# A fused convolution and two-token expert kernel: constants stored by piece, the router's two largest found together, longer weighting and transform sums, and a new order

## The chip, the cores and the metric

The kernel runs on one core of a Trainium2 chip. A core has five engines that run their own instruction streams: TensorE (PE, matmuls into PSUM), VectorE (DVE), ScalarE (ACT), GpSimd (POOL) and SyncE (SP, which here only issues DMAs). Engines meet through semaphores. The metric is device time in microseconds (us) of one execution, lower is better.

## The reference

`L` is 2048 tokens, `D` 512 channels, `NS` 128 states per channel. A gate `g` mixes two branches of the same input `u`: a long convolution (an S4 layer) and an expert layer that touches two tokens alone.

```python
dt = exp(log_dt)[:, None];  A = A_re + 1j * A_im
P  = exp((dt * A)[:, :, None] * l)                      # l = 0 .. L-1, per channel and state
K  = einsum("dn,dnl,dn->dl", C, P, dt * B).real         # kernel of the convolution, [D, L]
a  = irfft(rfft(pad(u)) * rfft(pad(K)))[:L] + u * Dskip # causal convolution over tokens

r   = x @ w_r;  idx = argsort(-r)[:2]                   # the two tokens with the largest logits
y   = (silu(x[idx] @ w_gate) * (x[idx] @ w_up)) @ w_down * sigmoid(r[idx])
b   = x.at[idx].add(y)

g   = sigmoid((u * gate_w).sum(-1))
out = g * a + (1 - g) * b                               # [1, 2048, 512] bf16
```

## The kernel before, in words

The kernel is a list of operations made by `P.add` (through the helpers `TT`, `TS`, `STT`, `CP`, `EV`, `AF`, `MM`, `DMA`), each with the buffers that it reads and writes. `PLAN` gives the order in which they are emitted, each with the alternative (mostly: which engine) that is used, and `BANKS` gives each PSUM tile its banks. `replay` and `emit_plan` turn that into one stream per engine, with a semaphore wait for every dependence that crosses engines. So every engine runs in the fixed order of `PLAN`, and one late operand holds up all that stands behind it on its engine. The costs in the helpers (`c_dve`, `issue`, `rate` and so on) describe operations to the planner that made `PLAN`; they emit nothing.

The channels go in two halves of 256 (`hf` or `c`, 0 and 1). The stages, with the names used below:

- **Parameters** (`nat0` to `nat5`, `ldt`, `al`, `bs`, `bn`, `bc`, `kw`, `k0`, and "polar"): the parameters are loaded, transposed on PE (`nt`, `nw`) and brought to modulus and phase. `hm` are 22 warm-up matmuls on a constant written by `one`.
- **Exponentials** (`ep`, `eq`, `ek` on ACT) give the moduli; `moduli` (`cm`) and `weigh` (`mw`, `mf`) multiply them up on DVE.
- **Coarse and fine waves** (`coarse`, `fine`): PE adds up a phase in PSUM (`pa`, L683 and L688), ACT takes its sine (`sin`, L437), and DVE multiplies by the moduli: `ns`, `pi`, `pr` for each of 4 coarse groups, `qm` (L729) for each of 5 fine groups G_. Each `qm` covers 2048 columns: real and imaginary plane of 1024.
- **Lags** (`lags`): PE multiplies coarse by fine waves (`kmm`, L925), which are evicted (`kae`), selected (`sel`, L939) and evicted again (`kce`, `kcx`, `k0c`). `kt` and `ku` make the tail terms.
- **Spectrum** (`spectrum`): PE multiplies the lags by the constant `c_near`, four pieces of 512 KB (`kn`, L1145; `ks`, L964), and `c_far` (`kf`, L969); the results are evicted (`khe`, `khf`).
- **Transform** of the input (`transform(m)`, m the block of 1024 tokens): PE multiplies tokens by the constant `c_fwd`, two pieces of 512 KB for odd and even tokens (`fl`, `fm`, L553; `fw`, L872). Evictions are `fwo` (scaled by -2, L861) and `fwe`. Two accumulating DMAs on POOL's queue (`vb`) and then DVE's `v1`, `v0`, `w1`, `w0` (L886 to L890) form the planes. `w1` and `w0` are four operations of 1024 columns per block, one for each plane.
- **Products and inverse** (`products(c, j)`, `inverse(c, j)`): DVE multiplies input and kernel spectra (`prod`) and sums them (`acc`, `yr`, `yi`, `pq`, `b0`, `b2`, `b13`), in places with the sums on PE (`ac`, L1032 to L1036, evicted by `ace`). PE does the inverse (`iv`, L1111 to L1116), with the second branch added through `rd` (the residual), and `ive` (L1127, L1131) evicts and weighs by the gate; `out` stores.
- **Rows** (L732 to L844): logits of the gate and the router come from a transposed load of the input (`xt`) by `wl` and `log`. The router follows, then the gather of its two tokens (`gu`), the expert (`wg`, `wu`, `wd`, `ff`, `dn`), `z1`, `bu`, and the scatter (`sc`) into `u_routed`, a copy of the input in device memory made by `uc`. From it `ue` and `u2` are loaded for `rd`'s matmuls.

The router before finds its two maxima one after the other (L776 to L783). `gmax` reduces 16 columns to one per partition (L769), spreads that over all partitions by a matmul (`gt`, L771) and reduces 128 columns (L772). For each of the two tokens it runs twice: for the logit, then for the index among the places where the logit is found (`cand`). Between the two tokens the first one's place is masked (`sel`, `mask`). Then `rs0`, `msb`, `ix0` (POOL) and `idx` (DVE) bring the logits to the sigmoid and the indices to an integer.

Half 0 of each stage runs ahead of half 1, with the transform and the rows between. On SP the input, `c_fwd`, the transposing load, the expert's weights, the constants of the spectrum and the stores follow each other in `PLAN`'s order.

## Time and profile before

| | |
|---|---|
| three runs | 148.18, 149.94 and 154.42 us; median 149.94 |
| profiled execution | 148.89 us, span of its instructions 146.8 us, mean granted TensorE clock 0.977 |
| bytes moved | 26.40 MB, mean 180 GB/s |
| engine instructions, busy | in the prediction below |

The page's strip of the span in 40 slices shows how full each engine is (a digit is the busy share in tenths, 9 is 90% or more):

```profile
PE   7964669999999959998999976599999998999992
PEld 3751363445446626665558664587788666877881
DVE  0789999889999989999999998999999979999943
ACT  4699999899999859888978777999968943358461
POOL 4000000604944583631500000000000000000000
PEclk9999985699999999999999999999999999999999
DMA  4799999995089992189970559248751000002155
```

PE is TensorE's matmuls and PEld its weight loads, which run beside them. Each digit stands for 3.67 us. A row such as `L408 DVE TENSOR_TENSOR RB<-RB 128x2048 bf16<-128x2048 bf16 x60 | 71.0, 1218 | ...` gives line, engine and operation, destination and source with partitions x elements, the count, the time in all (us), the mean of one (ns), and behind the second bar the idle time of the engine just before with what ended it. Nearly all buffers lie in one allocation, `RB`, so shapes and lines tell operations apart. L408, L414, L425, L428, L434 and L437 are lines of helpers that record many operations.

### The profile page before, as it was taken

Reading aid. Unit: us, or ns where it says so; the run is one execution under the profiler, and the core shown is the slowest. Engines: PE = TensorE matmul, PEld = TensorE weight load, DVE = VectorE, ACT = ScalarE, POOL = GpSimd, SP = SyncE. Lnnn points to the kernel's source line nnn. Section 1 sums busy time; section 2 is a strip of 40 time slices with the busy share of each in tenths; the row PEclk is TensorE's granted clock in tenths of the full one; section 3 lists DMA queues with packets and bytes.
Section 4 is the critical chain, followed back from the end, with each engine's and each line's share of the span. In section 5 each row is a group of like instructions: output and inputs, shape, how many; then the busy total and the mean of one; then the engine's idle time right before and its main releaser. Section 6 shows DMA issues by size and latency. Waiting matters only on the chain.

```text
span 146.8 us, 3150 instructions
## 1 busy us (share of the span) xinstructions
PE 129.1 (88%) x1302; PEld 89.1 (61%) x1309; DVE 132.9 (91%) x172; ACT 116.4 (79%) x165; POOL 25.6 (17%) x34
## 2 busy tenths in 40 slices
PE   7964669999999959998999976599999998999992
PEld 3751363445446626665558664587788666877881
DVE  0789999889999989999999998999999979999943
ACT  4699999899999859888978777999968943358461
POOL 4000000604944583631500000000000000000000
PEclk9999985699999999999999999999999999999999
DMA  4799999995089992189970559248751000002155
GB/s 133 208 264 262 292 220 357 408 401 228 9 133 180 193 369 63 36 241 262 474 333 29 156 94 424 110 136 291 289 108 49 0 4 0 0 0 76 38 168 154
DMA packets 23501, 26.40 MB, mean 180 GB/s; under 512 B 9208, under 2 KB 19840, under 8 KB 23328
## 3 DMA queue, kind: packets, MB, share of 16 engines
q1 hardware_dynamic: 20574, 23.03, 49.5%
q0 software_dynamic: 1136, 2.26, 8.9%
q10 hardware_dynamic: 1778, 0.92, 2.1%
q8 instruction: 10, 0.16, 0.5%
q14 instruction: 3, 0.02, 0.1%
HBM read 19.78 MB, written 4.20 MB: 163 GB/s over the span
## 4 chain that ended last, share of the span: by engine, by line
PE 40%; DVE 26%; DMA 11%; ACT 11%; SPq 4%; POOL 3%; issue 2%; ACTq 0%
DVE RB L408 20%; PE psm L1116 11%; DMA RB<-in_A_u_dram 8%; ACT RB L428 7%; PE psm L964 6%; ACT RB L437 4%; PE psm L939 4%; PE psm L872 3%; DMA RB<-c_near 3%; PE psm L925 3%; PE psm L1032 3%; PE psm L1111 2%; DVE RB L434 2%; POOL RB L414 2%; PE psm L746 2%
## 5 line engine op out<-in xcount | busy, mean ns | idle before, releaser
L408 DVE TENSOR_TENSOR RB<-RB 128x2048 bf16<-128x2048 bf16 (+12 forms) x120 | 112.5, 987 | 2.7 <-PE psm L1036 1.3
L428 ACT ACTIVATE RB<-psm 128x1024 bf16<-128x1024 f32 (+7 forms) x46 | 39.4, 872 | 10.7 <-PE psm L1036 6.2
L437 ACT ACTIVATE RB<-psm 128x1024 bf16<-128x1024 int16 (+1 forms) x37 | 36.4, 1020 | 4.5 <-PE psm L541 1.4
L872 PE MATMUL psm<-RB 128*128 128x512 bf16 x61 | 17.2, 419 | 6.3 <-DVE RB L861 3.2
L1116 PE MATMUL psm<-RB 128*128 128x256 bf16 x160 | 22.1, 273 | 0.0
L683 PE MATMUL psm<-RB 128*128 128x256 f16 (+1 forms) x112 | 20.7, 326 | 0.5 <-ACT RB L437 0.4
L437 ACT ACTIVATE RB<-RB 128x512 bf16<-128x512 f32 (+5 forms) x32 | 16.5, 590 | 3.0 <-POOL RB L414 1.8
L1116 PEld LDWEIGHTS psm<-RB 128*128 128x128 bf16 x160 | 15.6, 98 | 1.9 <-ACT RB L428 0.2
L1127 ACT ACTIVATE RB<-psm,RB 128x256 bf16<-128x256 f32 x27 | 10.9, 478 | 6.9 <-PE psm L1116 6.8
L964 PE MATMUL psm<-RB 128*128 128x256 bf16 x128 | 15.0, 273 | 1.0 <-DMA RB<-c_near 0.9
L683 PEld LDWEIGHTS psm<-RB 128*128 128x128 f16 x112 | 10.3, 97 | 8.7 <-ACT RB L437 0.9
L872 PEld LDWEIGHTS psm<-RB 128*128 128x128 bf16 x64 | 6.3, 105 | 14.6 <-DVE RB L861 4.0
L964 PEld LDWEIGHTS psm<-RB 128*128 128x128 bf16 x128 | 12.4, 98 | 3.6 <-DMA RB<-c_near 1.4
L688 PE MATMUL psm<-RB 128*128 128x512 f16 x44 | 13.0, 391 | 1.3 <-ACT RB L437 1.1
L925 PE MATMUL psm<-RB 128*128 128x80 bf16 x256 | 10.2, 198 | 2.3 <-DVE RB L408 1.6
L925 PEld LDWEIGHTS psm<-RB 128*128 128x128 bf16 x256 | 9.7, 96 | 3.7 <-ACT RB L428 3.4
L428 ACT ACTIVATE RB<-psm,RB 128x1024 bf16<-128x1024 f32 (+1 forms) x9 | 9.1, 1064 | 1.2 <-PE psm L969 1.2
L1111 PE MATMUL psm<-RB 128*128 128x256 bf16 x32 | 8.7, 273 | 0.0
L1032 PE MATMUL psm<-RB 128*128 128x512 bf16 x21 | 6.5, 380 | 0.7 <-ACT RB L428 0.6
L688 PEld LDWEIGHTS psm<-RB 128*128 128x128 f16 x44 | 3.6, 98 | 5.7 <-ACT RB L437 4.5
L422 POOL CAST RB<-RB 128x16 bf16<-128x16 f32 (+3 forms) x5 | 5.6, 1123 | 8.0 <-DVE RB L761 7.9
L414 POOL TENSOR_SCALAR RB<-RB 128x1 f32<-128x1 f32 (+3 forms) x5 | 6.5, 1291 | 0.3
(75 smaller groups left out, 123.0 us busy)
## 6 DMA issues: line engine op xcount, KB each, us to landing
RB<-in_A_u_dram SPq DMA_DIRECT2D x8, 256.0 KB, 5.8
RB<-RB POOLq DMA_DIRECT2D x4, 512.0 KB, 7.2
RB<-c_near SPq DMA_DIRECT2D x4, 512.0 KB, 5.7
RB<-c_inv SPq DMA_DIRECT2D x1, 2048.0 KB, 7.9
RB<-u_routed SPq DMA_DIRECT2D x2, 1024.0 KB, 6.0
RB<-in_B_w_gate_dram SPq DMA_DIRECT2D x1, 1792.0 KB, 12.0
RB<-in_B_w_up_dram SPq DMA_DIRECT2D x1, 1792.0 KB, 15.5
RB<-in_B_w_down_dram SPq DMA_DIRECT2D x1, 1792.0 KB, 9.4
```

Source lines behind the costliest of these rows:

```text
L408: return P.add(name, [(eng, c_dve(n, mode) if eng == DVE else 1.0, lambda h: h.tensor_tensor(out=o(), in0=a_(), in1=b_(), op=op))], rd, wr ...
L428: return lambda h: h.activation(out=o(), in_=a_(), func=ACTF.Copy, scale=scale() if callable(scale) else scale)
L437: return P.add(name, [(ACT, cost or c_act(n), lambda h: h.activation(out=o(), in_=a_(), func=func, scale=scale))], rd, wr, table=table, **kw)
L683: r = h.matmul(P32(t, 0, 0, 128, 256 * l0, (1, 256 * nl)), DGM(0, 128, (DD.index(d) + 2) * 128, (1, 128)), src(0, 128, col + hf * CW, (0, ...
L688: r = h.matmul(P32(t, b, 0, 128, 0, (1, 512)), DGM(0, 128, 0, (1, 128)), DGM(0, 128, 128 + c_, (0, 512)), start=False, stop=False, skip_gr ...
L872: x = h.matmul(P32(t, b, 0, 128, 0, (1, 512)), FM(0, 128, 2048 * par + 1024 * pl + 512 * i + 256 * q + 128 * b, (1, 128)), U(0, 128, ((m * ...
L925: x = h.matmul(P32(t, q // 6, 0, 128, (q % 6) * 80, (1, 80)), TPv(0, 128, ri * 16384 + c * 8192 + r * 128, (1, 128)), TQv(0, 128, c * 1024 ...
L964: x = h.matmul(P32(t, kt // 2, 0, 128, (kt % 2) * 256, (1, 256)), KN(0, 128, 2048 * KNP[2 * pl + hc] + 512 * g + 128 * kt, (1, 128)), KC[c ...
L1032: r = h.matmul(P32(t, kt, 0, 128, 0, (1, 512)), CI(0, 128, 0, (1, 128)), f(k, 0, 512), start=(k == 0 and hc == 1), stop=False, skip_group_ ...
L1111: h.matmul(o, RD(0, 128, (tb + 8) % 16 * 128, (1, 128)), UE[q](0, 128, r * 256, (1, 256)) if early else U2(0, 128, tb * D + c * CW, (1, 25 ...
L1116: x = h.matmul(o, G(0, 128, (pl * 4 + kt) * 1024 + (r * 2 + q) * 128, (1, 128)), PQ(0, 128, r * 1024 + kt * 256 + pl * 256 if quarter else ...
L1127: x = h.activation(out=OT[k](0, 128, ocol(q, r), (1, 256)), in_=P32(t, 0, 0, 128, q * 256, (1, 256)), func=ACTF.Copy, scale=SGF["gc"](0, 1 ...
```

## The change

1. **Constants stored by piece.** `c_fwd` was stored with 8 KB per partition, both pieces beside each other, and a piece was read as 4 KB rows with a pitch of 8 KB; now the pieces lie one behind the other, each 512 KB without gaps. Likewise `c_near`, whose four pieces were 4 KB rows with a pitch of 16 KB. Bytes, rows and destinations are the same.
2. **Router.** `top` finds the eight largest of 16 columns (`h.max`), spreads the first two by two matmuls, and finds the eight largest of the 256 columns: both maxima come in one pass. A second pass over `cand` finds both indices. Index constants are scaled so that the second logit's place differs by adding one; `sel` and `mask` are gone, and POOL gets `ix1` and `ix2`.
3. **Weighting.** `qm` is made for groups (0, 1), (2, 3) and (4): two operations of 4096 columns and one of 2048 for each half.
4. **Transform sums.** `w1` and `w0` are one operation of 2048 columns each, for both planes. To make the signs alike, `fw` takes the odd tokens of plane 0 in the other order.
5. **New order.** `PLAN` and `BANKS` are new: 546 operations instead of 560. Among what moves: `id0` stands ahead of `one` on POOL, nine instead of eight `hm` ahead of `dt`; ACT issues `fm` (odd), `nat5` and `nat2`, SP `nat1` and `dgb`; two `fwo` of block 1, `k0e` and one more `ive` go from ACT to DVE, `rd` of half 0, `log`, `rs` and one `k0c` from DVE to ACT; the last `qm` of half 0 stands behind `pi` and `pr` of half 1; `uc` stands ahead of `kf`, `u8` and `kn`; the first products of block (1, 1) stand among those of (0, 1).

Costs of POOL operations and rates of loads in the helpers are changed too; those are the planner's.

```diff
-    f_c = nc.inline_tensor(bf16_bits(fwd_mat()), "c_fwd").ap().bitcast(BF)
+    f_c = nc.inline_tensor(bf16_bits(fwd_mat().reshape(128, 2, 2048).transpose(1, 0, 2).reshape(256, 2048)), "c_fwd").ap().bitcast(BF)
-    kn_c = nc.inline_tensor(bf16_bits(near.reshape(128, NG, 2, 2, 512).transpose(0, 3, 2, 1, 4).reshape(128, 8192)), "c_near").ap().bitcast(BF)
+    kn_c = nc.inline_tensor(bf16_bits(near.reshape(128, NG, 2, 2, 512).transpose(3, 2, 0, 1, 4).reshape(512, 2048)), "c_near").ap().bitcast(BF)
...
-            DMA("fm", lambda h: [h.dma_start(FM(0, 128, 2048 * par, (1, 2048)), dr(f_c, 2048 * par, (4096, 128), (1, 2048)))], [], [bF[par]], 512, also=also, rate=180.0)
+            DMA("fm", lambda h: [h.dma_start(FM(0, 128, 2048 * par, (1, 2048)), dr(f_c, 2048 * 128 * par, (2048, 128), (1, 2048)))], [], [bF[par]], 512, also=also, rate=360.0)
...
-                q = lambda G_=G_: TQv(0, 128, hf * 10240 + G_ * 1024, (5120, 2), (1, 1024))
-                TT("qm", q, q, lambda G_=G_: MQ(0, 128, hf * 5120 + G_ * 1024, (0, 2), (1, 1024)), ALU.mult, bQS[G_][hf] + [bMW[hf] if G_ < 2 else bMF[G_][hf]], [bQF[G_][hf]], 2048)
+                for gs in ((0, 1), (2, 3), (4,)):
+                    if gs[-1] != G_:
+                        continue
+                    q = lambda gs=gs: TQv(0, 128, hf * 10240 + gs[0] * 1024, (5120, 2), (1, 1024 * len(gs)))
+                    TT("qm", q, q, lambda gs=gs: MQ(0, 128, hf * 5120 + gs[0] * 1024, (0, 2), (1, 1024 * len(gs))), ALU.mult, [x for g in gs for x in bQS[g][hf]] + [bMW[hf] if g < 2 else bMF[g][hf] for g in gs], [bQF[g][hf] for g in gs], 2048 * len(gs))
...
-        def gmax(src, bsrc, tag):
-            P.add("gm", [(DVE, 0.17, lambda h: h.tensor_reduce(out=RT["pm"](0, 128, 0, (1, 1)), in_=src(0, 128, 0, (1, 16)), axis=AX.X, op=ALU.max))], [bsrc], [bRT["pm"]])
+        def top(src, bsrc, tag):
+            P.add("gm", [(DVE, 0.17, lambda h: h.max(out=RT["pm"](0, 128, 0, (1, 8)), in_=src(0, 128, 0, (1, 16))))], [bsrc], [bRT["pm"]])
             t = P.pst(1, "gm")
-            MM("gt", lambda h, t=t: h.matmul(P32(t, 0, 0, 128, 0, (1, 128)), RT["pm"](0, 128, 0, (0, 128)), CF(0, 128, 0, (1, 128)), start=True, stop=True), [bRT["pm"], bCF], [t], 0.5)
-            P.add("gm2", [(DVE, 0.29, lambda h, t=t: h.tensor_reduce(out=RT[tag](0, 128, 0, (1, 1)), in_=P32(t, 0, 0, 128, 0, (1, 128)), axis=AX.X, op=ALU.max))], [t], [bRT[tag]])
+            def gt(h, t=t):
+                for k in range(2):
+                    r = h.matmul(P32(t, 0, 0, 128, 128 * k, (1, 128)), RT["pm"](0, 128, k, (0, 128)), CF(0, 128, 0, (1, 128)), start=True, stop=True)
+                return r
+            MM("gt", gt, [bRT["pm"], bCF], [t], 1.0)
+            P.add("gm2", [(DVE, 0.43, lambda h, t=t: h.max(out=RT[tag](0, 128, 0, (1, 8)), in_=P32(t, 0, 0, 128, 0, (1, 256))))], [t], [bRT[tag]])
...
-        for c in range(2):
-            m, v = "m%d" % (c + 1), "v%d" % (c + 1)
-            gmax(rb2, brb2, m)
-            STT("cand", row(cand, 0, 16), row(rb2, 0, 16), one1(m), idx, ALU.is_equal, ALU.mult, [brb2, bRT[m], bCF], [bcand], 16)
-            gmax(cand, bcand, v)
-            if c == 0:
-                TS("sel", row(cand, 0, 16), idx, one1(v), ALU.is_equal, [bRT[v], bCF], [bcand], 16, s2=-3.0e38, op1=ALU.mult)
-                TT("mask", row(rb2, 0, 16), row(cand, 0, 16), row(rb2, 0, 16), ALU.add, [bcand, brb2], [brb2], 16, 1)
+        top(rb2, brb2, "m1")
+        STT("cand", row(cand, 0, 16), row(rb2, 0, 16), one1("m1"), idx, ALU.is_ge, ALU.add, [brb2, bRT["m1"], bCF], [bcand], 16)
+        STT("cand", row(cand, 0, 16), row(rb2, 0, 16), two1("m1"), row(cand, 0, 16), ALU.is_ge, ALU.mult, [brb2, bRT["m1"], bcand], [bcand], 16)
+        top(cand, bcand, "v1")
...
-        TS("ix0", one1("ix0"), lambda: CF(0, 128, 147, (1, 1)), one1("v1"), ALU.mult, [bRT["v1"], bCF], [bRT["ix0"]], 1, s2=4096.0, op1=ALU.add, eng=POOL)
+        TS("ix0", one1("ix0"), lambda: CF(0, 128, 147, (1, 1)), one1("v1"), ALU.mult, [bRT["v1"], bCF], [bRT["ix0"]], 1, s2=lambda: CF(0, 128, 152, (1, 1)), op1=ALU.add, eng=POOL)
+        TS("ix1", one1("ix1"), two1("v1"), 1.0, ALU.is_ge, [bRT["v1"], bCF], [bRT["ix1"]], 1, s2=lambda: CF(0, 128, 153, (1, 1)), op1=ALU.mult, eng=POOL)
+        TT("ix2", one1("ix0"), one1("ix0"), one1("ix1"), ALU.add, [bRT["ix0"], bRT["ix1"]], [bRT["ix0"]], 1, 1, eng=POOL)
...
-                for i, r in enumerate((par + 2, par)):
+                for i in range(2):
                     for pl in range(2):
+                        r = par + 2 * (i == 0) if not (par and not pl) else par + 2 * i
...
-            for hc in (1, 0):
-                for pl in range(2):
-                    TT("w%d" % hc, vs(1, hc, pl, 512), vs(1, 0, pl, 512), xs(1 - pl, 512), ALU.add if pl == hc else ALU.subtract, [bVs[m][1][0][pl], bXO[m][1 - pl]], [bVs[m][1][hc][pl]], 1024)
+            ws = lambda hc: (lambda: V(0, 128, vo[m][1] + hc * 1024, (vo[m][3] - vo[m][1], 2), (512, 2), (1, 512)))
+            xw = lambda: XO[m](0, 128, 1024 * m + 512, (-1024 if m else 1024, 2), (-512, 2), (1, 512))
+            TT("w1", ws(1), ws(0), xw, ALU.subtract, bVs[m][1][0] + bXO[m], bVs[m][1][1], 2048)
...
+                TT("w0", ws(0), ws(0), xw, ALU.add, bVs[m][1][0] + bXO[m], bVs[m][1][0], 2048)
...
-            DMA("kn", lambda h, i=i: [h.dma_start(KN(0, 128, 2048 * KNP[i], (1, 2048)), dr(kn_c, 2048 * i, (8192, 128), (1, 2048)))], [], [bKN[i]], 512, rate=330.0)
+            DMA("kn", lambda h, i=i: [h.dma_start(KN(0, 128, 2048 * KNP[i], (1, 2048)), dr(kn_c, 2048 * 128 * i, (2048, 128), (1, 2048)))], [], [bKN[i]], 512, rate=370.0)
```

46 lines of the change are left out of this document (29 added, 17 removed), and 68 rows, old and new, of the table PLAN.

## The prediction, as it was put on record

> **What bounds the kernel now.** First the page's busy times, then the table of stretches, to see whether one engine carries the whole run or each stage has its own bound.
>
> ```profile
> PE 129.1 (88%) x1302; PEld 89.1 (61%) x1309; DVE 132.9 (91%) x172; ACT 116.4 (79%) x165; POOL 25.6 (17%) x34
> ```
>
> ```profile
> 5.00:25.00 20.00, 14.27 (x128) 8.79 (x128) 19.25 (x34) 19.70 (x33) 0.00 (x0) 0.90 1.03 265
> ...
> 60.00:80.00 20.00, 18.83 (x294) 12.64 (x293) 19.45 (x23) 17.07 (x22) 5.18 (x7) 1.00 0.78 252
> ...
> 100.00:115.00 15.00, 14.71 (x157) 11.76 (x156) 14.93 (x19) 13.06 (x26) 0.00 (x0) 1.00 0.54 178
> ...
> 130.00:140.00 10.00, 10.00 (x84) 7.91 (x84) 9.86 (x11) 6.38 (x14) 0.00 (x0) 1.00 0.19 54
> ```
>
> VectorE (DVE) is busy for 132.9 of 146.8 us, and no stage gives it a rest: 19.25 of 20 us early, 9.86 of 10 near the end. But it is not alone. ScalarE (ACT) is full in the first stretch (19.70 of 20), and TensorE (PE) is full in the last two (14.71 of 15, 10.00 of 10). So two engines at a time are full: DVE with ACT first, DVE with PE later. Work that moves from one of the full ones to another gives nothing; a wait taken out of DVE's row, or DVE work removed outright, gives time.
>
> So the third view is what DVE waited for:
>
> ```profile
> DVE RB L408 <- PE psm L574: 5.1, 2, 4.5
> DVE RB L1131 <- PE psm L1116: 2.2, 3, 1.3
> DVE RB L408 <- PE psm L1036: 1.3, 2, 1.0
> DVE RB L772 <- PE psm L771: 0.7, 1, 0.7
> DVE RB L408 <- ACT RB L428: 0.6, 1, 0.6
> DVE RB L843 <- POOL RB L412: 0.4, 1, 0.4
> DVE RB L408 <- ACT RB L437: 0.2, 1, 0.2
> ```
>
> Of these, 4.5 us is the start (no input has come yet) and 2.2 us the last evictions of the inverse, after the last product. Between lie 0.6 (the rest of L574) + 1.3 + 0.7 + 0.6 + 0.4 + 0.2 = 3.8 us. These 3.8 us are all that a better order could win on DVE between its first and its last product.
>
> Where DVE's last product ends, and what follows, is in DVE's timeline (start, length):
>
> ```profile
> 124.98 15.48 DVE L408 TENSOR_TENSOR RB<-RB 128x2048 bf16<-128x2048 bf16 x15 [0.33 <-PE psm L1036]
> ...
> 144.03 0.42 DVE L1131 TENSOR_TENSOR RB<-psm,RB 128x256 bf16<-128x256 f32 x1 [0.18 <-PE psm L1116]
> ```
>
> The last sum of products ends at 124.98 + 15.48 = 140.5; from there to 146.8 are 6.3 us of inverse matmuls, eviction and store. The chain of waits shows how the second half of the channels gets to PE:
>
> ```profile
> 72.46 2.72 PE psm L939 x36
> ...
> 80.85 4.58 DMA RB<-c_near
> ...
> 93.34 2.62 PE psm L925 x68
> ...
> ```
>
> ```profile
> 100.79 2.62 PE psm L939 x36
> ...
> 105.81 3.49 PE psm L964 x32
> ```
>
> The selection of half 0 (L939) starts at 72.5. The lag matmuls of half 1 (L925) start at 93.34, its selection at 100.8, its spectrum (L964) follows from 105.5 on. From 93.3 PE is the chain nearly to the end, with DVE full beside it.
>
> **The change part by part: DVE's work.** Durations by shape (mean ns of one; busy time divided by the count is what one costs in a row, since neighbours overlap):
>
> ```profile
> L408 DVE TENSOR_TENSOR RB<-RB 128x2048 bf16<-128x2048 bf16 x60 | 71.0, 1218 | 0.9 <-PE psm L1036 0.3 <-ACT RB L437 0.2
> ...
> L408 DVE TENSOR_TENSOR RB<-RB 128x1024 bf16<-128x1024 bf16 x31 | 20.1, 684 | 0.1
> ...
> L408 DVE TENSOR_TENSOR RB<-RB 128x4096 bf16<-128x4096 bf16 x4 | 9.1, 2284 | 1.6 <-PE psm L1036 1.0 <-ACT RB L428 0.6
> ...
> L772 DVE TENSOR_REDUCE RB<-psm 128x1 f32<-128x128 f32 x4 | 1.1, 286 | 0.7 <-PE psm L771 0.7
> ...
> L769 DVE TENSOR_REDUCE RB<-RB 128x1 f32<-128x16 f32 x4 | 0.7, 163 | 0.0
> ...
> L425 DVE SCALAR_TENSOR_TENSOR RB<-RB 128x16 f32<-128x16 f32 x2 | 0.5, 230 | 0.0
> ...
> L414 DVE TENSOR_SCALAR RB<-RB 128x16 f32<-128x16 f32 x1 | 0.2, 228 | 0.0
> ...
> L408 DVE TENSOR_TENSOR RB<-RB 128x16 f32<-128x16 f32 x1 | 0.2, 176 | 0.0
> ```
>
> Weighting (qm): per half, five operations of 2048 become two of 4096 and one of 2048. One costs 71.0/60 = 1.18, the long one 9.1/4 = 2.28, so a merge saves 2 x 1.18 - 2.28 = 0.09, four of them 0.35 us. Transform sums (w1, w0): eight of 1024 become four of 2048: 2 x 20.1/31 - 1.18 = 0.11 each, 0.45 us. The merged access keeps rows of 512 with step 1, as the single ones had; I take the rate of the 2048 row. Were the longer pattern at half that rate, four would cost 4.7 more; nothing in the rows speaks for it. PE's order of the forward matmuls flips one plane's sign, at the same count: nothing.
>
> Router: removed are 4 x 0.163 + 4 x 0.286 + 2 x 0.230 + 0.228 + 0.176 = 2.67 us; added are two eight-largest searches over 16 columns, two over 256, and two of the 0.230 kind. A search by max appears nowhere in the trace. Nearest rows are the reductions: 0.163 for 16 columns, 0.286 for 128, that is 1.1 ns a column, so 0.43 for 256. Low end 0.29 each, high end 0.86 (two passes); I take 0.43, since a reduction reads the same columns. Sum 2 x 0.163 + 2 x 0.43 + 0.46 = 1.65: 1.0 saved, 0.1 to 1.3 between the ends. PE has the same four products of 128 columns.
>
> The new order then moves work between DVE and ACT:
>
> ```profile
> L861 DVE TENSOR_SCALAR RB<-psm 128x1024 bf16<-128x1024 f32 x3 | 3.6, 1213 | 0.0
> ...
> L1131 DVE TENSOR_TENSOR RB<-psm,RB 128x512 bf16<-128x512 f32 x2 | 1.4, 692 | 2.0 <-PE psm L1116 2.0
> ...
> L1161 DVE TENSOR_TENSOR RB<-RB 128x1024 bf16<-128x1024 bf16 x1 | 1.2, 1207 | 0.0
> ...
> L434 DVE CAST RB<-psm 32x512 bf16<-32x512 f32 x1 | 0.7, 696 | 0.1
> ```
>
> ```profile
> L1127 ACT ACTIVATE RB<-psm,RB 128x256 bf16<-128x256 f32 x27 | 10.9, 478 | 6.9 <-PE psm L1116 6.8
> ...
> L1159 ACT ACTIVATE RB<-RB 128x128 bf16<-128x128 bf16 x8 | 2.4, 396 | 0.0
> ```
>
> DVE takes two evictions of transform 1 (L861, 2 x 1.21), k0e (0.69, by its 512-column sister L434) and one more inverse eviction (0.69 in two of 512 against two of 0.478 on ACT), and gives up the residual (L1161, 1.21; on ACT it is eight operations, 2.4 us). Three copies of at most 256 columns go to ACT too; I count them at nothing, behind work that fills both engines, and their loss of cover would cost under a microsecond. Sum on DVE: -0.35 - 0.45 - 1.0 + 2.4 + 0.7 + 0.7 - 1.2 = +0.8 us in all; ahead of the last product, where three instead of two and a half evictions no longer count, about +0.3. So the work that was saved is spent again, and the time hangs on waits.
>
> **The waits.** Start: the constant that the warm-up matmuls read is now written after a larger memset, and one more warm-up stands before dt.
>
> ```profile
> 0.72 0.20 POOL L525 MEMSET RB<- 128x128 bf16 x1 [0.29 <-POOLq L1228]
> 0.86 0.31 POOL L526 MEMSET RB<- 128x256 bf16 x1
> ...
> ```
>
> ```profile
> 0.99 1.89 PE L537 MATMUL psm<-RB 128*128 128x256 bf16 x8 [0.99 <-POOL RB L525]
> ```
>
> That is 0.31 + 1.89/8 = 0.5 us later for dt, for ACT's exponentials and for DVE's first operation. The later wait for L574 (0.6) is of the same size as before. Loads: on SP two issues fewer stand before the transposing load, so it starts about a microsecond earlier; ACT issues one c_fwd piece and two parameter loads in their place, while it waits for dt. dgb goes from POOL to SP, behind a load that nobody awaits then. The copy to u_routed is now issued before c_far, u8 and c_near: these wait anyhow for transform 1 to leave their buffers, so it fills time that was empty. The second u2 piece and kt stand further back on SP; the first is read by the last inverse only, the second by ku, which DVE reaches some 5 us after.
>
> The c_near and c_fwd pieces become contiguous in memory; a row of 4 KB stays one row. The last piece now takes 4.58 us (80.85 row). Bounds: 5.6 and 3.6, a microsecond to either side, since the trace holds no such pair. I take 4.58: the bytes and the rows are the same. It matters little: in the new order the product that awaited the fourth piece (0.6 us on ACT L428) stands behind one long qm more.
>
> Half 0 comes later: in DVE's row its last qm, which its lag matmuls await, now stands behind two more coarse groups of half 1 (pi and pr, 4 x 1.18, and two short negations), about 5 us of work. PE then does those matmuls in one go instead of in pieces between sines; I put selection 0 at 74 instead of 72.5.
>
> Main gain: half 1. In DVE's row between bu and the last qm of half 1 stood four qm, two products of 4096, the residual and one yr: 4 x 1.18 + 2 x 2.28 + 1.2 + 1.18 = 11.7 us. Now they are two long qm, one product, one short qm: 3 x 2.28 + 1.18 = 8.0. DVE thus allows L925 to start 3.7 us earlier; ACT, whose last sine of half 1 has 1.9 us less work ahead (two evictions moved off, the residual moved on, three spectrum evictions moved behind), allows about 2. I take 2.5 for L925, L939 and the first L964: 90.8, 98.2, 103. What comes of it at the end is less: PE has one inverse of half 0 more behind L939 (ten matmuls of 256 columns, 1.1), and the first product of the last block stands about 7 us earlier in DVE's row, right behind that spectrum: I allow 1.1 us of wait there. The waits between DVE's first and last product then are 0.5 (start of kw, L574) + 0.5 (router) + 0.6 (L1036, half of now) + 1.1 = 2.7 against 3.8.
>
> Tail: after the last b13 come two inverse blocks of ten and eleven matmuls and four of another (25 x 0.109 = 2.7), an eviction (0.7) and the store (146.8 - 144.45 = 2.35): 5.8 against 6.3.
>
> Sum against the profiled execution (148.89 us, span 146.8): start +0.5, work +0.3, waits -1.1, tail -0.5 = -0.8. PE comes out alike: 2.5 earlier at L939, 1.1 more work behind it, which leaves room for 0.6 of waiting. Time 148.1 us. The median of the three runs shown is 149.94, 0.7% above the profiled one.
>
> [...] Two POOL steps (ix1, ix2) are added between the maxima and the index.
>
> ```profile
> 51.56 2.62 POOL L414 TENSOR_SCALAR RB<-RB 128x1 bf16<-128x1 f32 x1
> 54.26 0.24 POOL L412 TENSOR_SCALAR RB<-RB 128x16 f32<-128x16 f32 x1
> ```
>
> ```profile
> 51.78 2.35 DVE L408 TENSOR_TENSOR RB<-RB 128x2048 bf16<-128x2048 bf16 x2
> ```
>
> A one-column step took 2.62 us while DVE ran two long operations, 0.24 when DVE stood still. Between the last maximum and idx DVE has ns, blo, one cm, pi and pr, about 4.7 us; three POOL steps at 2.62 would need 7.9. But once DVE stands at idx the rest take 0.24 each: two are through by 5.2, the third by 5.5, so the price is 0.8 us, 0 if one step takes 1.3. [...]
>
> **The rivals.** (1) Forecast, 148.1: chance 0.38. (2) Nothing gained: the moved work and the POOL steps eat the head start, 148.9 to 150; for it, +0.8 on DVE and full engines everywhere; against it, the 3.7 us at half 1. Chance 0.15. (3) All middle waits go: 148.89 - 3.8 + 0.5 + 0.3 - 0.5 = 145.4, and 144.5 with the router at its low end and the exponentials not late; for it, that every wait named is a matter of order; against it, that a new order makes new waits. Chance 0.27. (4) Slower: DVE runs into the first products of the last block before ACT has their spectrum.
>
> ```profile
> 114.18 3.12 ACT L428 ACTIVATE RB<-psm,RB 128x1024 bf16<-128x1024 f32 x3
> ```
>
> ACT's last eviction for them ended at 117.3. In the new DVE row about 106 us of work stand ahead of the product that needs it, with 7 us of start and waits: it is reached at 113, so a spectrum as late as before makes 4.0 us of wait where I allow 1.1: 148.1 + 2.9 = 151.0. Each microsecond that L964 starts after 105.5 adds one; from 106.5 on it is over 2% slower, 152 and more. For it: half 0 comes later, and its spectrum's evictions stand ahead of half 1's on ACT. Against: the 3.7 us by which DVE lets L925 start earlier. Chance 0.20.
>
> **How the numbers follow.** Two per cent, about what a measurement of this kernel can tell, is 3.0 us: faster is below 145.9, slower above 151.9. Faster 0.27 (rival 3), same 0.53 (1 and 2), slower 0.20 (4). The range 144.5 to 151.5 takes in rival 3 and the mild end of 4, and leaves out about 0.2 (half of 4 and the best of 3); the forecast's own range is 146.5 to 149.5.
>
> **What would show it.** Right: DVE busy 133 to 134 us with 14 instructions fewer; L925 of half 1 at about 91, first L964 of half 1 at 103; searches of 256 columns at 0.43; first DVE operation at 5.0; selection 0 at 74; the last product at about 140.2. Wrong: L964 after 105.5, a DVE wait of over 2 us for ACT's L428 between 105 and 115, a wait at idx of over 1 us, w at 2.3 us.

## The result, and the profile after

| | before | after |
|---|---|---|
| median of four runs on one chip | 149.06 us (148.07 to 154.42) | 154.11 us (152.96 to 155.03) |
| profiled execution, its span | 148.89, 146.8 | 152.96, 151.1 |
| TensorE clock granted in it | 0.977 | 0.953 |

The changed kernel is slower: after / before 1.036, 95% interval 1.025 to 1.046. The forecast was 148.1 in a range of 144.5 to 151.5; the measured time lies above it, so the forecast was wrong. (Medians here and below are over all executions; ratios compare undisturbed executions alone, so they need not be the quotient of the medians.)

The helpers' lines have moved by three to nineteen: L411 is the two-input VectorE operation (L408 before), L440 ScalarE's sine (L437), L431 its copy (L428), L686 and L691 the phases `pa`, L834 `dn`, L870 `fwo`, L882 `fw`, L944 `kmm`, L958 `sel`, L983 `ks`. First the page's busy times and the clock's strip:

```profile
PE 132.0 (87%) x1302; PEld 89.9 (60%) x1309; DVE 134.3 (89%) x158; ACT 116.4 (77%) x171; POOL 26.8 (18%) x35
...
PEclk9999857999999997589999999999999999999999
```

VectorE (DVE) has 14 instructions fewer and 1.4 us more work. TensorE's clock has a second dip, in slices 16 to 18 (57 to 68 us), which the strip of before does not have. Next, what DVE waited for (in all, times, longest):

```profile
DVE RB L411 <- PE psm L577: 4.9, 1, 4.9
DVE RB L411 <- ACT RB L440: 2.4, 1, 2.4
DVE RB L411 <- DMA RB<-RB: 1.8, 1, 1.8
DVE RB L711 <- ACT RB L440: 1.6, 1, 1.6
DVE RB L1150 <- PE psm L1135: 1.4, 3, 0.6
DVE RB L428 <- POOL RB L411: 0.5, 1, 0.5
```

With three more waits of 0.2 us, and without the start (4.9) and the tail (1.4), that is 6.9 us, where before had 3.8 and the forecast 2.7. Three waits make 5.8 of it: 1.6 and 2.4 for sines, 1.8 for `vb`, the accumulating DMA. The chain of waits (start, length, what) shows how they hang together:

```profile
58.05 1.61 PE psm L834 x56
59.67 0.88 PE psm L691 x2
...
60.76 1.49 PE psm L882 x3
62.25 0.85 PE psm L691 x2
63.10 2.45 PE psm L686 x12
...
65.58 0.89 ACT RB L440
...
66.50 3.77 ACT RB L440 x4
70.27 0.93 ACT RB L431
...
71.49 9.72 DMA RB<-RB
```

`dn` (L834) begins at 58.05, phases and sines follow, the last `fwe` (L431) at 70.27 and with it `vb` at 71.49, landed at 81.2. Before, that `vb` was issued at 62.3:

```profile
62.31 1.27 POOL L885 DMA_DIRECT2D RB<-RB  x1 [0.80 <-ACT RB L428]
```

TensorE's timeline of after says what preceded `dn`; the bracket is the idle time before the row:

```profile
54.91 1.02 PE L686 MATMUL psm<-RB 128*128 128x512 f16 x4
58.05 1.61 PE L834 MATMUL psm<-RB 128*128 128x2 bf16 x56 [2.12 <-POOL RB L417]
...
62.90 4.37 PE L686 MATMUL psm<-RB 128*128 128x256 f16 x20
```

2.12 us with nothing, then 20 phase matmuls in 4.37 us. The releaser named, a POOL operation that ends at 58.0, belongs to the gate. The products that `dn` reads were made on POOL by 52.9:

```profile
50.13 2.77 POOL L411 TENSOR_TENSOR RB<-RB 128x28 bf16<-128x28 bf16 x2 [3.55 <-ACT RB L440]
```

The load of `dn`'s weights `w_down`, issued at 48.4, took 9.6 us and landed at 57.9: of `dn`'s own inputs it came last (in e3 below the same wait, 2.1 us, is put down to that load). Before, TensorE had a wait of 1.65 us, and 22 phase matmuls took 2.79:

```profile
54.78 0.81 PE L872 MATMUL psm<-RB 128*128 128x512 bf16 x3 [1.65 <-ACT RB L428]
55.46 2.79 PE L683 MATMUL psm<-RB 128*128 128x256 f16 x22
```

In after's trace the clock changes at 17.50, 24.32, 58.45 and 65.28 us, which lie 6.82, 34.13 and 6.83 us apart: 2, 10 and 2 times 3.41. The table of stretches of that length shows it (busy time and count of PE, PEld, DVE, ACT and POOL, then the clock, the DMA share and GB/s; the clock is third from the end), first after, then before:

```profile
55.04:58.45 3.41, 1.29 (x21) 0.62 (x19) 3.41 (x5) 2.25 (x3) 2.56 (x3) 1.00 1.64 667
58.45:61.87 3.42, 3.20 (x51) 1.92 (x50) 1.85 (x2) 2.01 (x3) 1.78 (x1) 0.50 0.11 43
61.87:65.28 3.41, 3.41 (x15) 2.00 (x14) 3.34 (x4) 1.02 (x1) 0.00 (x0) 0.50 0.00 0
65.28:68.69 3.41, 3.10 (x15) 1.20 (x14) 1.68 (x2) 3.11 (x4) 0.00 (x0) 1.00 0.00 0
```

```profile
51.80:55.21 3.41, 1.76 (x10) 0.69 (x8) 3.00 (x5) 1.61 (x4) 2.62 (x2) 1.00 1.09 368
55.21:58.63 3.42, 3.42 (x27) 2.46 (x26) 3.42 (x4) 3.42 (x6) 1.17 (x2) 1.00 0.17 52
```

After, TensorE was busy for 1.29 of 3.41 us, and the clock stood at 0.50 for the next 6.8 us. Before, with its wait of 1.65 us at 53, was busy for 1.76 of 3.41, and the clock stayed. These rows show what followed what, not why; in e7 below, with the wait filled, the clock stayed at 1.00.

At the end nothing is lost or won: the last sum of products ends at 127.54 + 17.22 = 144.8, and 6.3 us follow, as before.

```profile
127.54 17.22 DVE L411 TENSOR_TENSOR RB<-RB 128x2048 bf16<-128x2048 bf16 x19
```

So the 4.3 us between the spans are DVE's work (+1.4), its waits (6.9 - 3.8 = +3.1) and the start (4.9 against 4.5), less 0.8 in the tail's waits, within 0.3.

### The profile page after: what moved, and what is told of

Read it like the earlier page. It is cut to its first block, busy times and chain, and to the rows that moved or that the text cites. A ratio compares the mean times of both kernels' runs of the same rounds, so it can differ in the third digit from the quotient of the medians.

```text
span 151.1 us, 3145 instructions
## 1 busy us (share of the span) xinstructions
PE 132.0 (87%) x1302; PEld 89.9 (60%) x1309; DVE 134.3 (89%) x158; ACT 116.4 (77%) x171; POOL 26.8 (18%) x35
## 4 chain that ended last, share of the span: by engine, by line
PE 37%; DVE 31%; ACT 13%; DMA 9%; POOL 5%; issue 2%; SPq 1%
DVE RB L411 21%; PE psm L1135 11%; ACT RB L431 8%; DMA RB<-RB 6%; PE psm L983 6%; ACT RB L440 4%; POOL RB L417 4%; PE psm L1051 3%; DVE RB L870 3%; DMA RB<-in_A_C_re_dram 3%; PE psm L686 2%; PE psm L1130 2%; PE psm L1055 2%; PE psm L1053 2%; PE psm L958 2%
## 5 line engine op out<-in xcount | busy, mean ns | idle before, releaser
L411 DVE TENSOR_TENSOR RB<-RB 128x2048 bf16<-128x2048 bf16 (+8 forms) x111 | 111.8, 1054 | 5.5 <-ACT RB L440 2.4
L431 ACT ACTIVATE RB<-psm 128x1024 bf16<-128x1024 f32 (+8 forms) x44 | 36.9, 858 | 16.1 <-PE psm L1055 11.0
L440 ACT ACTIVATE RB<-psm 128x1024 bf16<-128x1024 int16 (+1 forms) x37 | 36.3, 1021 | 8.6 <-PE psm L686 3.1
L686 PE MATMUL psm<-RB 128*128 128x256 f16 (+1 forms) x112 | 22.3, 351 | 0.2 <-ACT RB L440 0.2
L882 PE MATMUL psm<-RB 128*128 128x512 bf16 x60 | 16.7, 410 | 4.1 <-DVE RB L870 3.1
L440 ACT ACTIVATE RB<-RB 128x512 bf16<-128x512 f32 (+5 forms) x32 | 16.8, 594 | 1.1 <-DVE RB L411 1.1
L983 PE MATMUL psm<-RB 128*128 128x256 bf16 x128 | 15.1, 272 | 2.5 <-DVE RB L437 2.5
L686 PEld LDWEIGHTS psm<-RB 128*128 128x128 f16 x112 | 11.5, 107 | 9.1 <-ACT RB L440 1.2
L691 PE MATMUL psm<-RB 128*128 128x512 f16 x44 | 14.4, 415 | 0.9 <-ACT RB L440 0.9
L983 PEld LDWEIGHTS psm<-RB 128*128 128x128 bf16 x128 | 12.5, 98 | 4.2 <-issue 2.6
L882 PEld LDWEIGHTS psm<-RB 128*128 128x128 bf16 x64 | 6.0, 104 | 13.2 <-DVE RB L870 4.9
L1146 ACT ACTIVATE RB<-psm,RB 128x256 bf16<-128x256 f32 x25 | 10.1, 479 | 2.3 <-PE psm L1135 1.8
L944 PE MATMUL psm<-RB 128*128 128x80 bf16 x256 | 10.5, 198 | 1.2 <-DVE RB L411 0.7
L944 PEld LDWEIGHTS psm<-RB 128*128 128x128 bf16 x256 | 9.8, 96 | 2.7 <-DVE RB L411 1.2
L411 POOL TENSOR_TENSOR RB<-RB 128x1 f32<-128x1 f32 (+4 forms) x6 | 4.6, 773 | 31.9 <-DVE RB L782 24.2
L431 ACT ACTIVATE RB<-psm,RB 128x1024 bf16<-128x1024 f32 (+1 forms) x9 | 9.4, 1071 | 0.0
L417 POOL TENSOR_SCALAR RB<-RB 128x1 f32<-128x1 f32 (+3 forms) x6 | 7.6, 1310 | 3.6 <-DVE RB L782 3.5
L1051 PE MATMUL psm<-RB 128*128 128x512 bf16 x21 | 6.5, 380 | 0.8 <-ACT RB L431 0.4
L691 PEld LDWEIGHTS psm<-RB 128*128 128x128 f16 x44 | 3.5, 102 | 5.9 <-ACT RB L440 4.0
## 6 DMA issues: line engine op xcount, KB each, us to landing
RB<-in_B_w_gate_dram SPq DMA_DIRECT2D x1, 1792.0 KB, 10.4
```

The costliest lines, as they stand in the source:

```text
L411: return P.add(name, [(eng, c_dve(n, mode) if eng == DVE else 1.4, lambda h: h.tensor_tensor(out=o(), in0=a_(), in1=b_(), op=op))], rd, wr ...
L417: f = lambda h: h.tensor_scalar(out=o(), in0=a_(), scalar1=s1() if callable(s1) else s1, scalar2=s2() if callable(s2) else s2, op0=op0, op ...
L431: return lambda h: h.activation(out=o(), in_=a_(), func=ACTF.Copy, scale=scale() if callable(scale) else scale)
L440: return P.add(name, [(ACT, cost or c_act(n), lambda h: h.activation(out=o(), in_=a_(), func=func, scale=scale))], rd, wr, table=table, **kw)
L686: r = h.matmul(P32(t, 0, 0, 128, 256 * l0, (1, 256 * nl)), DGM(0, 128, (DD.index(d) + 2) * 128, (1, 128)), src(0, 128, col + hf * CW, (0, ...
L691: r = h.matmul(P32(t, b, 0, 128, 0, (1, 512)), DGM(0, 128, 0, (1, 128)), DGM(0, 128, 128 + c_, (0, 512)), start=False, stop=False, skip_gr ...
```

## The experiments

Most kernels below keep the changed kernel's code and change its `PLAN`; their helper lines lie four further down than after's (L415, L444, L948). An order is given by the operations' names.

**Content or order?** e1 has all four edits of content in before's order: `PLAN` of before, less the operations that are gone, a merged operation at the place of the last one it replaces.

```diff
-PLAN = [(2, 0), (1, 0), (0, 0), (6, 0), (5, 0), (7, 0),
+PLAN = [(1, 0), (7, 0), (8, 0), (9, 0), (10, 0), (11, 0),
...
```

> All four edits of content of the changed kernel (pieces, router, merged qm, merged w), in the order of the kernel before: its plan with the operations that are gone left out, a merged operation at the place of the last it replaces. Theory O (the new order costs the time): 147.5 to 149.5 us, that is, no slower than before, the transform of block 1 stored by about 61 us as before, its accumulating DMA vb of about 7 us. Theory C (one of the edits of content costs it, by longer VectorE operations that hold others up): 152 us or more.

151.24 us, ratio 1.021 (1.013 to 1.029). Neither theory: in before's order the content costs about 2%. That the new order costs the rest does not follow from this: the intervals of e1 and of the changed kernel (1.025 to 1.046) overlap, and e10 below has the same content, with matmuls that nothing reads beside it, at 1.010. DVE's and TensorE's timelines of e1:

```profile
50.50 0.43 DVE L715 TENSOR_SCALAR RB<-RB 128x1024 bf16<-128x1024 bf16 x1 [1.38 <-ACT RB L444]
50.84 3.42 DVE L415 TENSOR_TENSOR RB<-RB 128x4096 bf16<-128x4096 bf16 x2
```

```profile
62.40 0.46 PE L948 MATMUL psm<-RB 128*128 128x80 bf16 x8 [1.80 <-DVE RB L415]
62.70 1.03 PE L690 MATMUL psm<-RB 128*128 128x512 f16 x4
63.56 3.30 PE L948 MATMUL psm<-RB 128*128 128x80 bf16 x48
```

DVE waits for a sine where before it had the first half of a `qm` to do; then it does both halves in one, and comes to the last `qm` of half 0 0.9 us later than before. TensorE, which before came to the lag matmuls 0.5 us after that was done, waits 1.80 us, and its clock falls: 48 lag matmuls take 3.30 us, 1.89 before.

**What in the new order?** e2 moves `dn`:

```diff
-PE: pa(coarse1) dn pa(coarse1) fw pa(fine1) ... pa(coarse1) fw kmm
+PE: pa(coarse1) pa(coarse1) fw ... pa(coarse1) fw dn pa(fine1) pa(fine1) pa(fine1) kmm
```

> The changed kernel with one group moved: dn (the w_down product) and what depends on it (its copy z0, the first sines and phases of fine1) stand on TensorE and ScalarE behind the last transform product and its store fwe, where the kernel before has dn too. Theory D (dn stands on TensorE ahead of its weights, stops the phases behind it, and so makes ScalarE's sines, the last fwe and vb late): TensorE's wait of 2.1 us ahead of dn goes, fwe by 66 us in place of 70.1, VectorE's waits of 1.57 and 2.42 us for L440 shrink below 1.5 us in sum, its wait of 1.84 us for vb goes, 149 to 151 us. Theory U (the early copy uc holds up w_down and vb): vb still takes over 9 us, 152 to 154 us. If the dip of TensorE's granted clock at 60 to 70 us comes from its stop ahead of dn, the dip goes too.

157.08 us, ratio 1.058 (1.054 to 1.061), which neither theory had. DVE's three waits go, but the phases of fine1 now stand between `dn` and the lag matmuls, one sine apart each, and DVE waits 8.96 us in one piece for L948. And the wait at 56 us is still there (2.02 us, for a sine): `dn` filled part of it. The clock did not recover either: it stood at half from 58.4 to 61.8 and from 68.6 to 78.9 us, so part of the 8.96 us is the clock's. The lag matmuls of e2 (56 of them took 2.19 us in after):

```profile
74.42 3.94 PE L948 MATMUL psm<-RB 128*128 128x80 bf16 x56
```

e3 moves the copy `uc` on SP.

```diff
-SP: wd cib uc kf u8 kn kn kn tm kn
+SP: wd cib kf u8 kn kn kn uc tm kn
```

> The changed kernel with the copy of u (uc, L850) moved on SyncE behind the third c_near piece, about where the kernel before has it; nothing else. Theory U: w_down lands 2 us or more earlier, vb of block 1 takes about 7 us in place of 9.7, 150 to 151.5 us. Theory D: w_down lands less than 1 us earlier and dn still waits, 152.5 to 154 us. Both are to be had in part.

161.54 us (158.8 to 164.5): theory U falls. Without `uc` beside them, `w_down` took 9.5 us (9.6 in after) and `vb` 9.75 (9.72). The loss is new. The third `kn` waits on SP for its buffer until 83.6 us, as in after; `uc` now stands behind it and goes out at 84.0, and the last `kn` of 512 KB lands beside it in 10.6 us (median 5.0 in after):

```profile
86.63 10.63 DMA RB<-c_near
```

TensorE waits 3.8 us for that `kn`. DVE loses more elsewhere: the scatter waits for `uc`, which lands at 95.7, and the DMA of the tail terms `kt` stands behind the scatter on SP. It goes out at 98.3 us, at 89.6 in after, and DVE waits 6.9 us for it:

```profile
DVE RB L415 <- DMA RB<-RB: 8.7, 2, 6.9
```

Behind 55 us, the clock of e3's trace stood at half in three stretches (58.4 to 65.2, 85.7 to 89.1 and 95.9 to 102.7 us), where after has the first alone.

e4 has both moves, the two diffs together.

> Both moves of the two runs before in one kernel. If the two causes are all of it: 147.5 to 149.5 us, no slower than the kernel before. If a third part of the new order costs as well (the chain of half 0 interleaved later on VectorE, the last qm of half 0 late): over 150.5 us.

164.97 us, ratio 1.112 (1.106 to 1.118): the two losses add up (3.0 and 7.4 us above after's median, 10.9 together). DVE waits 7.8 us for L948 as in e2, and 7.5 us for `kt` as in e3.

e5 tries to fill the wait with the transform itself:

```diff
-PE:  pa(coarse1) dn pa(coarse1) fw pa(fine1) pa(fine0) ... fw kmm kmm
+PE:  pa(coarse1) fw pa(coarse1) pa(fine0) pa(coarse1) fw pa(fine0) dn pa(coarse1) kmm kmm pa(fine1) kmm ...
-DVE: qm ns pi pr fwo pr qm
+DVE: qm fwo ns pi pr pr qm
```

> The changed kernel with a stretch of its order rewritten: the last transform product of block 1 fills TensorE's wait ahead of dn, its store fwo goes on VectorE into the place of the 1.57 us wait, the second product and the store fwe follow at once, dn stands behind them, and the phases of fine1 stand among the lag products instead of ahead of them. Theory W (the three waits of VectorE, 1.57, 2.42 and 1.84 us, are what the new order costs; two come from phases behind dn, one from the late fwe and so the late vb): fwe by 64 us in place of 70.1, vb landed by 76, the three waits together under 2 us, 147.5 to 150 us. Rival (the loss would turn up again on TensorE or ScalarE, as in the run that only moved dn): 152 us or more.

157.26 us (154.19 to 158.42): the rival, since even the shortest execution is as long as after. In its trace `vb` goes out at 66.0 us and DVE no longer waits for it, but waits 6.3 us for the lag matmuls, which again stand behind phases that wait for their sines. The clock stood at half from 67.2 to 74.0 us, and part of that wait may be the clock's. In this order, bringing one chain forward put another behind.

e7 leaves the order alone and puts 20 matmuls into the wait ahead of `dn`:

```diff
+        twf = P.pst(1, "wf")
+        def wf(h):
+            r = None
+            for _ in range(20):
+                r = h.matmul(P32(twf, 0, 0, 128, 0, (1, 256)), CI(0, 128, 0, (1, 128)), CI(0, 128, 0, (1, 256)), start=True, stop=True)
+            return r
+        MM("wf", wf, [bCIA], [twf], 2.0)
...
```

> The changed kernel with 20 matmuls of 256 columns on the identity put on TensorE into its wait ahead of dn, about 2 us that nothing reads. Theory K (the wait of 2.1 us with nothing on TensorE lets the granted clock fall to 0.5 for 6.8 us, and the phases at half speed make the later waits): no segment at 0.5 between 55 and 75 us, the phases at 60 to 67 us at their full speed, 150 to 152 us. Rival (order alone sets the waits; the slow clock is hidden): the clock stays full and the time at 153 to 155 us.

153.11 us, ratio 1.030 (1.019 to 1.040), by time not told from after. In its trace the clock holds (1.00 from 56.05 to 66.29 us), the 20 phase matmuls take 3.29 us in place of 4.37, and the wait of 2.4 us is gone. The other two stay, and a wait of 1.0 us at 12 us for the gate's logits (L747) is new, behind the load of their weights:

```profile
DVE RB L415 <- DMA RB<-RB: 1.7, 1, 1.7
DVE RB L715 <- ACT RB L444: 1.6, 1, 1.6
DVE RB L1154 <- PE psm L1139: 1.4, 3, 0.6
DVE RB L438 <- PE psm L747: 1.0, 1, 1.0
```

e9 mends two places: the phase and sine of coarse1 ahead of `dn`, and the last sum of block 0 ahead of the one that waits for `vb`. e10 is e9 with e7's matmuls.

```diff
-PE:  pa(coarse1) dn pa(coarse1) fw          ACT: sin z0 sin(fine1) sin(coarse1)
+PE:  pa(coarse1) pa(coarse1) dn fw          ACT: sin sin(coarse1) z0 sin(fine1)
-DVE: w1(block 0) v0(block 1) w0(block 0)
+DVE: w1(block 0) w0(block 0) v0(block 1)
```

> The changed kernel with two places mended: the phases of coarse1 and their sine that stood behind dn on TensorE and ScalarE stand ahead of it (dn loses 0.9 us), and on VectorE the second weighting of block 0, whose inputs are long there, stands ahead of the operation that waits for vb. Theory W: the wait of 1.57 us falls below 0.5, that of 1.84 us to about 0.6, the wait of 2.42 us behind the slow clock stays; 150.8 to 152.5 us. Rival (what is mended in one place is waited for in the next): 153 to 155 us.

> The two places of e9 and the 20 idle matmuls of e7 in TensorE's wait. Theory W with K (the three waits and the clock are all that the new order costs): no segment at 0.5 between 55 and 75 us, the wait of 2.42 us below 1 us, 149 to 151 us, between the kernel before and e1. Rival: no better than e7, 152 to 154 us.

e9: 152.37 us, ratio 1.019 (1.011 to 1.027). e10: 150.37 us, ratio 1.010 (1.005 to 1.014). The same place in DVE's timeline, e9 first, then e10:

```profile
71.26 1.23 DVE L415 TENSOR_TENSOR RB<-RB 128x2048 bf16<-128x2048 bf16 x1 [4.23 <-ACT RB L444]
```

```profile
68.34 1.23 DVE L415 TENSOR_TENSOR RB<-RB 128x2048 bf16<-128x2048 bf16 x1 [1.59 <-ACT RB L444]
```

The wait of 1.57 us is gone in both; in e9 the next one grows to 4.23, with the clock at half from 60.7 to 67.5 us in its trace (of an execution of 153.73 us, one of its longer ones). With the matmuls that nothing reads, in the same order, the clock holds (20 phase matmuls take 3.20 us; the mean granted clock is 0.989, 0.966 in e9) and 1.59 is left, where below 1 was expected: between these two traces 2.6 us of the wait go with the clock. The wait for `vb` falls to 0.50 us in e10. By time, e9 and e10 are not told apart, since their intervals overlap; so what the filling is worth by itself is not settled. Together the two moves and the filling take the changed kernel from 1.036 (1.025 to 1.046) to 1.010 (1.005 to 1.014), intervals apart, and so recover most of what it lost. What makes up the last per cent is open.

**What in the content?** e6 is e1 with `qm` in five parts; e8 is the kernel before with the merged `qm` alone; e11 has pieces and router alone (one plane of the odd tokens enters `w` with the other sign there; operations, sizes and order are before's).

```diff
-                for gs in ((0, 1), (2, 3), (4,)):
-                    if gs[-1] != G_:
-                        continue
...
+                TT("qm", q, q, lambda G_=G_: MQ(0, 128, hf * 5120 + G_ * 1024, (0, 2), (1, 1024)), ALU.mult, bQS[G_][hf] + [bMW[hf] if G_ < 2 else bMF[G_][hf]], [bQF[G_][hf]], 2048)
```

e8 is the reverse of this diff on the kernel before. e11 takes e6 and undoes `w`:

```diff
...
-            TT("w1", ws(1), ws(0), xw, ALU.subtract, bVs[m][1][0] + bXO[m], bVs[m][1][1], 2048)
...
+            for hc in (1, 0):
+                for pl in range(2):
+                    TT("w%d" % hc, vs(1, hc, pl, 512), vs(1, 0, pl, 512), xs(1 - pl, 512), ALU.add if pl == hc else ALU.subtract, [bVs[m][1][0][pl], bXO[m][1 - pl]], [bVs[m][1][hc][pl]], 1024)
```

> The content of the change in the order of the kernel before, as in e1_old_order, but qm in its five parts as before (pieces, router and merged w stay). Theory Q (in the old order the merged qm puts its first half, which filled VectorE's wait for a ScalarE sine, on the path behind that wait, and so the first lag product 1 us later): the wait of 1.38 us at 50 us is filled again, TensorE's wait of 1.80 us ahead of the lag products and the dip of its granted clock at 64 us go, 147.5 to 149 us. Rival (merged w, router or pieces cost the time): 150.5 to 151.5 us, no change from e1_old_order.

> The kernel before with one edit alone: qm merged (three operations in place of five for each half), a merged operation at the place of the second. Theory Q: VectorE waits 1 us or more at 50 us, the first lag product begins 0.7 us or more later, 149.8 to 151.5 us, although VectorE's work is about 0.4 us less. Rival: 148 to 149 us, as the kernel before or a little less.

> Old order with two edits of content alone, the pieces and the router; qm and w as before. Theory A (the router's 1 us on VectorE is taken up by a wait for ScalarE's sines near 50 us, merged w neither gains nor loses): 148 to 150 us, as before and as e6. Rival L (merged w costs as merged qm does): 147 to 148.5 us, faster than e6 by 1 us or more.

| | median, us | ratio to before |
|---|---|---|
| e1, all content | 151.24 | 1.021 (1.013 to 1.029) |
| e6, `qm` apart | 150.23 | 1.004 (0.998 to 1.010) |
| e8, merged `qm` alone | 150.49 | 1.014 (1.001 to 1.027) |
| e11, pieces and router | 149.06 | 1.001 (0.996 to 1.005) |

In before's order the merged `qm` costs 1 to 2%: e1 and e6 differ by it, with intervals apart, and e8 comes out longer than before although DVE's work falls by 0.5 us (132.9 to 132.4). The path of theory Q is seen in e1 and in e6, whose trace has neither the wait at 50 us nor the dip at 64. It is not seen in e8: its trace (of its shortest execution, 149.44) has a wait of 1.1 us at 50, but its lag matmuls begin earlier than in before, so how e8 loses its per cent is in no trace. And e6 came out at 150.23, longer than theory Q's 147.5 to 149. e6 and e11 are no faster than before, with 0.4 and 0.2 us less work. In both traces the clock stood at half for 3.4 us near 95 us, behind a wait of TensorE of 2.1 us, and DVE has a new wait; in e11 (lines of e11, whose trace is of its longest execution, 151.50):

```profile
DVE RB L415 <- DMA RB<-RB: 2.3, 1, 2.3
```

**Where the rest of the gain may go.** In e11's trace the later `vb` landed 17.1 us after its issue, at 79.0. In before it took 14.5 and landed at 76.8, and nobody waited: DVE came to it at 77.1. In these two traces a head start of DVE would end there. `uc` is issued at 67.6 in before, at 67.2 in e11, and runs beside `vb`'s packets. e13 is pieces and router in before's order (with before's `fw`), and `uc` early:

```diff
-SP: wd kn cib kn kf kn uc tm kn
+SP: wd uc kn cib kn kf kn tm kn
```

> Old order, pieces and router (qm and w as before), and the copy uc issued on SyncE right behind w_down, where the changed kernel has it. Theory V (uc's packets beside vb's hold the last of vb's up, and VectorE's gain of about 1 us ends in the wait for them): vb's last packet ends by 73 us, no wait of VectorE for it, 146.8 to 148.3 us, at least 0.5% faster than the kernel before. Rival (the last packets are late for another reason): they end at 76 to 79 us as in e11, 148.5 to 149.5 us.

148.13 us, ratio 0.995 (0.991 to 1.000). DVE no longer waits for `vb`, which takes 11.4 us and lands at 73.5. The table of e13's `vb` (the last line is issue to landing, shortest, middle, longest of two):

```profile
DMA to landing us min/median/max: 5.6/8.5/11.4
```

The time moves by half a per cent, at the edge of what these runs resolve, and e13's interval overlaps e11's. Nor is it shown that the copy is what held `vb` up: with `uc` at 65.6 to 67.6 us the later `vb` took 14.5 us (before), 16.5 (e6), 17.1 (e11) and 11.9 (e12), with `uc` early 11.4 (e13), 11.3 (e14), 11.6 (e15) and 10.4 (e16). The traces of e12 and e15, which differ only in the place of `uc`, have nearly the same.

e12, e14, e15 and e16 put 16 idle matmuls into TensorE's wait near 53 us, in before, in e13, in before with `uc` early, and in e13 with merged `w`:

```diff
...
+            for _ in range(16):
+                r = h.matmul(P32(twf, 0, 0, 128, 0, (1, 256)), CI(0, 128, 0, (1, 128)), CI(0, 128, 0, (1, 256)), start=True, stop=True)
...
```

> The kernel before with 16 matmuls of 256 columns on the identity in TensorE's wait of 1.65 us at 53 us, which nothing reads. [...]

> e13 with the 16 idle matmuls of e12 in TensorE's wait near 53 us. Theory V with K: 146.8 to 148 us and no execution above 150. Rival: as e12, 148 to 149.

> The kernel before, no content of the change, with uc issued right behind w_down and the idle matmuls of e12. Theory V: vb's last packet earlier, but VectorE comes to it no earlier than before, so no gain over e12: 148 to 148.6 us. Rival (the move of uc itself is worth something): 147.5 us or less.

> Old order, pieces, router and merged w, qm apart, uc early and the idle matmuls. If the merged w gains its 0.45 us once vb is in time: 0.2 to 0.5 us below e14. If a merged w (2.4 us in two operations) comes later for those who need its first half: 0.3 us or more above e14.

| | median, us | ratio to before |
|---|---|---|
| e12 | 148.54 | 0.998 (0.994 to 1.002) |
| e14 | 150.18 | 0.998 (0.993 to 1.004) |
| e15 | 148.68 | 0.998 (0.994 to 1.003) |
| e16 | 148.41 | 0.999 (0.995 to 1.003) |

None of these is told from before by its ratio, so the early `uc` by itself and the merged `w` are worth less than can be seen here. What e12 may change is the spread: eleven of its twelve executions lie between 148.1 and 151.0, while 8 of 29 of the kernel before, on the same chip, lie above 151.2. (One execution each of e12, e6 and e15, at 701.8, 214.6 and 255.7 us, stands by itself and is unexplained.) Eleven executions are few for that, and e13, without idle matmuls, has none above 149.3, so the filling is not shown to be what narrows the spread. It would fit waits that now and then halve the clock; no trace of a long execution of before was at hand, so this is argued, not shown. e14 comes out longer than expected: seven of twelve lie at 150 to 151. In its trace matmuls are slow behind another wait, 2.15 us at 32 us (four phase matmuls at 36.79 us take 1.91 us, 1.02 in e10 at 56.37):

```profile
34.26 1.88 PE L690 MATMUL psm<-RB 128*128 128x512 f16 x10 [2.15 <-ACT RB L444]
```

The best version by the median is e13: 148.13, no execution above 149.3, where the kernel before on the same chip had 149.73 (147.9 to 154.6). e16 is close behind (148.41, also none above 149.3).

## Why the prediction was wrong

**Right in kind and size.** The start (first DVE operation forecast at 5.0, seen at 4.87), the search (0.43 against 0.423), the merged operations' rates, POOL's price at `idx` (0 to 0.8 us against 0.5), and DVE's 14 instructions. The rows of the new kernel, by shape:

```profile
L411 DVE TENSOR_TENSOR RB<-RB 128x4096 bf16<-128x4096 bf16 x8 | 18.1, 2286 | 0.1
...
L782 DVE MAX8 RB<-psm 128x8 f32<-128x256 f32 x2 | 0.8, 423 | 0.0
```

The last c_near piece, forecast at 4.58 us, took 4.1, inside the bounds (4.6 before). `uc` early "fills time that was empty": right, by e3.

**Two terms mis-sized.** The router was to save 1.0 us of DVE's work (0.1 to 1.3). e13 has 0.4 less than before, e11 0.2. The sum took the means of the small operations; in a row they overlap their neighbours, each by about 0.08 us (in before's trace an operation of 0.24 us that starts at 49.05 is followed by one at 49.21). Twelve such operations went and six came, so about 0.5 us of the 1.0 was never there, by that estimate. `qm` (0.35 forecast, 0.5 in e8) and `w` (0.45; e16 has 0.5 less than e13) were right. The 0.6 us that the router lacks is what DVE's work came out above the forecast (+1.4 against +0.8). The tail was to save 0.5 us and took 6.3 as before.

**The step that failed: the waits.** "The waits between DVE's first and last product then are ... 2.7 against 3.8". They were 6.9. The forecast followed the order around half 1's lag matmuls and gave the stretch from 55 to 82 us one sentence (half 0 comes later). There it overlooked two things.

First, TensorE's row. `dn` was moved ahead of phases of coarse1 and the transform's last products, to a place where neither its weights nor the sine for the phase behind it are there yet. The working followed moves on DVE and SP and not the move of `dn` on TensorE. Selection 0 came at 78.3, not 74, the last `fwe` nine us later than before, and so `vb`, which had no slack.

Second, the clock. The forecast took TensorE's durations from rows at full clock. Behind the wait of 2.1 us the clock stood at half for 6.8 us (20 phase matmuls took 4.37 us, 3.29 in e7, where the wait is filled). In the traces of e7 and of the pair e9 and e10 that goes with 2.4 and 2.6 us of DVE's wait; by time neither is told apart singly. The profile of before has an early dip of the clock, at 21 to 28 us; the working does not speak of it.

Both moves together with the filling (e10) recover most of the loss; the share of each is not resolved.

**The gain at half 1.** DVE did shorten its stretch to the lag matmuls: from selection 0 to L944 of half 1 it is 17.1 us, 20.9 before, 3.8 shorter where the forecast had 3.7. But it started late: L944 of half 1 at 95.4 us where 91 was forecast, L958 at 103.0 (98.2), the spectrum's L983 at 107.9 (103). Rival 4 named that figure, "from 106.5 on it is over 2% slower, 152 and more", and the time agrees by luck, since its mechanism was absent: there was no wait for ACT's L428 between 105 and 115. DVE itself was late by then, and from 81 to 145 us it waited for 0.2 us in all.

**Merged `qm`.** The forecast gave -0.35 us and no loss. In before's order it costs 1 to 2%; in e1's trace the first of two operations had been the filling of a wait. What it costs in the new order was not tried.

## What to carry to other kernels

Before merging two operations into a longer one, look whether the first of them fills a wait: the merged one begins when its last input is there (in e1, behind a wait of 1.38 us). For each move, read what stands next on the *same* engine and when its own inputs land, on every engine; an engine far from full can still set the time, since one late operand holds all behind it (in e3 SP's DMA of `kt` went out at 98.3 us, at 89.6 in after). Look at TensorE's clock behind its waits: here it stood at 0.50 after stretches of 3.41 us in which TensorE was busy for 1.29 (after) and 1.61 us (e1), and 20 phase matmuls took 4.37 us in place of 3.29. Matmuls that nothing reads can fill the wait (e7, e10), and whether that pays in time has to be measured.
